# A planner that also books PSUM banks when it works backwards, and three more units turned on TensorE

## The chip, the core and the metric

The program runs on one core of one Trainium2 chip. The engines are TensorE (PE in the profile, with its weight loads as PEld), VectorE (DVE), ScalarE (ACT), GpSimd (POOL) and SyncE (SP, which here only issues transfers). The metric is the device time of one execution in microseconds, as a median of several runs. For the kernel before it is 1066.04 us over three runs (1065.69 to 1067.02).

## The reference, cut to what matters

Three layers follow one another. The first is a linear recurrence over 768 time steps for 4 batches of 8 heads, with a complex decay per channel; the second and third are feed-forward layers over the 3072 tokens that come out of it, the third behind a root-mean-square norm.

```python
mag = np.sqrt(a_re * a_re + a_im * a_im)
scale = np.minimum(mag, 0.999) / (mag + 1e-06)
a_re_n, a_im_n = (a_re * scale, a_im * scale)
for t in range(S):                                   # 768
    new_re = ar * S_re - ai * S_im
    new_im = ar * S_im + ai * S_re
    S_re, S_im = (new_re + k_t (x) v_t, new_im)      # 48 x 48 per batch and head
    y[:, :, t] = q_t @ S_re
x = y as 3072 x 384
h = x @ w_in                                         # 384 x 2048
g = np.where(h >= 1, h, np.where(h <= -1, 0.0, (h + 1) ** 2 / 4))
x = g @ w_out                                        # 2048 x 384
xn = x / sqrt(mean(x * x) + 1e-06) * rms_g
g, val = xn @ w_gate, xn @ w_val                     # 384 x 1536 each
out = (g * sigmoid(g) * val) @ w_out2                # 1536 x 384
```

## The kernel before, in words

The 3072 tokens are cut into 12 **units**: two pairs of batches times six chunks of 128 time steps. A unit has two halves b = 0 and 1, one for each batch of its pair, so 256 tokens. Every float32 product is made of three float16 products (high by high, high by low, low by high), so that each tile has a high and a low part (`wi_h`, `wi_l`, `gmh`, `gml` and so on).

A unit passes through these stages:

- **The chain** (`attn`, up to `chain = plan.stage`): the decays of 128 steps are normalised and multiplied up to running products, channels by rows. ACT squares the input (`X<-a`), then DVE does some 70 to 90 instructions on `X`, `pr`, `C`, `K`, `E` and ends with two products and two sums (`a<-X,E`, `X<-a`). There is one tile `X`, so the chain of a unit cannot begin before the unit ahead of it has been read out of `X`.
- **The transposes of X** (`onto_tokens`): six float32 transposes on PE for each half, `bank<-idt,X`. Those of half 1 are the last reader of `X`.
- **Factors, scores, y, state**: DVE and ACT make k and q with their decays (`qhi`, `qlo`, `khi`, `klo`). These are turned, either by a DMA transpose from SP's queue or by a product with minus the identity on PE (`turned`: `bank<-nid,khi`, then an ACT copy `khT<-bank`). Then PE makes scores, `y` and the state of the recurrence. The result is split (`nh`, `nl`) and turned into `xTh`, `xTl`.
- **M1 and M2** (`moe1`, `moe2`): the two feed-forward layers. Each has a first product into a PSUM bank (`bank<-xTh,wi_h` for M1, `bank<-xnh,wv` for M2), an activation by ACT and DVE ending in `gmh` and `gml`, and a second product into an accumulator (`acc<-wo_h,gmh`, `acc<-w,gmh`).

In the first fifth of the run the weights arrive as 64-bit floats and are decoded by DVE, split by ACT and PE (`wv<-w`, `spt<-w`, `tmp<-spt` on DVE; `bank<-wv,idt`, `bank<-spt,w` on PE). Later, ACT reads the weights once more for range checks (`spt<-spt,e`).

No engine chooses its order at run time. A recorded program of operations is planned by `Plan.best`, and every engine then runs its list in order. The planner works in three steps. `order` is a list scheduler: it walks forward in time and gives each engine the ready operation that is due first (`op.late`); it also hands out the PSUM banks and the `tmp` buffers (`SHARED`), in turns by use and within the limits `CAPS`. `latest` is the backward walk that sets the due times: it runs the plan from its end with the durations of `cost`. In the kernel before, `latest` knows nothing of banks and buffers. `best` repeats the two `ROUNDS` times (once before) and adds a table of offsets, `SHIFT`, by stage name. `PEW` is a table that says for which units which step is done on PE instead of elsewhere: `'add'` means that the last sum of the chain is done by PE, which adds two float32 products in the bank (unit 1 before); `'k'` is the low part of k by PE; `'t'` is the turning of q and k, `'x'` of the layer input and `'n'` of the normed input on PE. `RATES`, `AHEAD1`, `STEP1`, `STEP2` and `CHECKS` set how the operations are interleaved when they are recorded, which decides ties and turns.

All operations are issued from one line (456 in the profile of the kernel before), so in the profile one goes by tile names.

Of the kernel before, what the change touches and what calls it, by code (L numbers as in the profile page):

```python
# [45 lines left out]
}  # L46
TOKS = 2

PEW = {'add': [1], 'sum': [], 'k': [2], 'q': [], 'p': [], 'g': [], 'm': [], 't': [0], 'x': [], 'n': []}

SHIFT = {'w1a': 12, 'm23': 12, 't40': -12, 'm22': 2, 'w2': 25, 't30': -1, 'c2': 3, 'y21': 5, 'c3': -1}
ORDER = [(1, 0), (1, 1), (2, 0), (2, 1), (1, 2)]
RATES = [14.7, 0, 40.2, 27.7, 29.4]
RATE = 0.62
AHEAD1, STEP1, STEP2 = 4, 5, 6
LAG = 3
CHECKS = 12
SWITCH = 8
BACKLOG = 1.5
SHARED = ('bank', 'tmp')  # L60
CAPS = {'mo': 4, 'at': 4, 'w': 4, 'n': 2, 'mo_': 3, 'at_': 3, 'w_': 2, 'out_': 1, 'one_': 1}
ROUNDS = 1
LAT = {'V': 0.13, 'A': 0.145, 'G': 0.1, 'T': 0.0, 'S': 0.0}
XLAT = {'V': 0.13, 'A': 0.145, 'G': 0.1, 'T': 0.2, 'S': 0.0}

# [9 lines left out]
def kw_rows(args, kw):  # L75
    return args[1].shape[0] / P
# [6 lines left out]
class Plan:  # L83
# [92 lines left out]
    def add(self, variants):  # L176

        keys = list(variants)
        name, args, kw = variants[keys[0]]
        aps = [(i, x) for i, x in enumerate(args) if hasattr(x, "ap") and hasattr(x, "offset")]  # L180
        outs = [kw["out"]] if "out" in kw else []
        ins = [x for n, x in kw.items() if n not in ("out", "accum_out") and hasattr(x, "ap") and hasattr(x, "offset")]
        for i, x in aps:
            (outs if i == 0 and "out" not in kw else ins).append(x)
        if kw.get("accum_out") is not None:
            outs.append(kw["accum_out"])
        if name == "matmul" and not kw["start"]:
            ins.append(outs[0])
        n = 1
        for d in list((outs[0]).shape)[1:]:  # L190
            n *= d
        alts = {key: self.cost(key, x[0], n, x[1], x[2], ins) for key, x in variants.items()}
        calls = {key: [x] for key, x in variants.items()}
        table = {AF.Abs_reciprocal_sqrt: 1, AF.Silu: 2}.get(args[2]) if name == "activation" else None
        mm = None
        if "T" in variants:
            f32 = args[1].dtype == F32
            mm = (300 if name == "transpose" else 6 + n * (4 if f32 else 1), kw_rows(args, kw))
        port = sum(x.space != PSUM for x in ins) > 1
# [55 lines left out]
    def cost(key, name, n, args, kw, ins):  # L255
# [12 lines left out]
            return 0.06 + n * {"tensor_tensor": 2.12e-3, "scalar_tensor_tensor": 3.75e-3, "memset": 1.1e-3}.get(name, 3.6e-3)  # L268
        if key == "T":
            f32 = args[1].dtype == F32  # L270
            return 0.4167e-3 * (300 if name == "transpose" else 6 + n * (4 if f32 else 1))
        return 1.25 if "transpose" in name else 0.4

    def best(self):
# [24 lines left out]
    def latest(self, res):  # L299

        ops = self.ops
# [2 lines left out]
            prio[i] = t + ops[i].alts[k]  # L304
        left = [len(op.succs) for op in ops]
        ready = [0.0] * len(ops)
        free = {k: 0.0 for k in self.engines}
        wait_q = {k: [] for k in self.engines}
        av_q = {k: [] for k in self.engines}
        eng = [next(iter(op.alts)) for op in ops]  # L310
        for op in ops:
            if not left[op.idx]:
                heapq.heappush(wait_q[eng[op.idx]], (0.0, op.idx))
        n = 0
        while n < len(ops):
# [12 lines left out]
                heapq.heappush(a, (-prio[i], i))  # L328
            if not a:
                continue  # L330
            op = ops[heapq.heappop(a)[1]]
            n += 1
            c = op.alts[k]
            st = t + (op.dma + 2.0 if op.dma else 0.0) + c
            free[k] = t + max(op.dma, c) if op.dma else st
            op.late = -st
            for p in op.preds:
                ready[p] = max(ready[p], st + (LAT[eng[p]] if eng[p] == k else XLAT[eng[p]]))
                left[p] -= 1
                if not left[p]:  # L340
                    heapq.heappush(wait_q[eng[p]], (ready[p], p))
        first = min(op.late for op in ops)
        for op in ops:
            op.late -= first

    def products(self, op, t):

# [8 lines left out]
    def order(self):  # L356
# [22 lines left out]
        while len(res) < len(ops):  # L379
# [22 lines left out]
                late, i = heapq.heappop(a)  # L402
            op = ops[i]
            new = [v for v in op.tiles if v not in held]
            lack = [v[0] for v in new if not spare[v[0]]] + [v[3] for v in new if turns.get(v[3], 0) != v[4] or using.get(v[3], 0) >= CAPS[v[3]]]
            if lack:
                stuck.setdefault(lack[0], []).append(i)
                continue
# [1042 lines left out]
```

## Time and profile before

| | kernel before |
|---|---|
| median of three runs | 1066.04 us |
| the profiled execution's own time | 1067.5 us |
| span of the profiled execution | 1065.8 us |
| PE busy | 995.5 us, 93% |
| DVE busy | 817.2 us, 77% |
| ACT busy | 812.7 us, 76% |
| mean granted clock of TensorE | 0.974 |

The span is the time from the first to the last instruction; the execution's own time is 1.7 us longer. Busy shares are averages over very different stages. In the first 200 us the weights are prepared; from about 360 us on, one unit after another goes through the same stages until the chain work runs out.

### The profile page before, as it was taken

The numbers are of one execution on the slowest core, as the hardware profiler recorded it, in microseconds if no ns is written. First come the engines' busy times: TensorE is split into PE (matmuls) and PEld (weight loads), VectorE is DVE, ScalarE is ACT, GpSimd is POOL, SyncE is SP. The second block draws the span as 40 slices with busy tenths as digits, with TensorE's granted clock in tenths as the row PEclk, the third lists the DMA queues.
The fourth block names the chain that finished last, engine by engine and source line by source line (L and its number), as shares of the span: only waits on it lengthen the run. The fifth ranks groups of instructions, "written<-read, shape, count | busy, mean of one in ns | idle before, by whom it ended". The sixth has DMA issues, their size and how long they took to land.

```text
span 1065.8 us, 23000 instructions
## 1 busy us (share of the span) xinstructions
PE 995.5 (93%) x9224; PEld 775.2 (73%) x9224; DVE 817.2 (77%) x1721; ACT 812.7 (76%) x1585; POOL 16.7 (2%) x27
## 2 busy tenths in 40 slices
PE   3577998998997899999999999999999999999996
PEld 1355866876875688778777787787887787877874
DVE  9989889979869889698797697896996984633321
ACT  6469879867787798899877897978978989946221
POOL 2000000000000000000000000000000000000000
PEclk9878998999998999999999999999999999999999
DMA  7563265256444443444335526336444321210000
GB/s 255 193 208 121 48 192 138 73 148 159 130 105 123 118 126 94 138 107 105 103 90 147 141 62 168 84 102 169 108 132 139 78 73 36 48 24 16 16 9 26
DMA packets 156018, 115.87 MB, mean 109 GB/s; under 512 B 135296, under 2 KB 138368, under 8 KB 155904
## 3 DMA queue, kind: packets, MB, share of 16 engines
q1 hardware_dynamic: 155904, 114.33, 40.0%
q8 instruction: 74, 1.21, 0.4%
q14 instruction: 40, 0.33, 0.1%
HBM read 77.07 MB, written 4.72 MB: 77 GB/s over the span
## 4 chain that ended last, share of the span: by engine, by line
PE 68%; DVE 16%; ACT 7%; DMA 4%; issue 4%; POOL 0%; SPq 0%; DVEq 0%; ACTq 0%
PE bank L456 43%; PE acc L456 25%; DVE tmp L456 3%; DVE X L456 3%; DVE pr L456 2%; ACT tmp L456 2%; DVE wv L456 2%; DMA w<-in_moe_w_out_dram 1%; ACT L456 1%; DMA spt<-in_moe_w_in_dram 1%; DVE gml L456 1%; DMA qvk<-in_qvk_t_dram 1%; ACT S L456 1%; DVE a L456 1%; ACT X L456 1%
## 5 line engine op out<-in xcount | busy, mean ns | idle before, releaser
L456 DVE SCALAR_TENSOR_TENSOR tmp<-bank,tmp 128x512 f32<-128x512 f32 (+1 forms) x184 | 117.0, 639 | 102.9 <-ACT tmp L456 56.2
L456 PEld LDWEIGHTS <-gmh 128*128 128x128 f16 x1344 | 130.1, 98 | 76.4 <-issue 10.6
L456 PE MATMUL bank<-xTh,wi_h 128*128 128x256 f16 (+1 forms) x672 | 169.1, 262 | 5.2 <-DVE S L456 2.6
L456 PE MATMUL bank<-xTl,wi_h 128*128 128x256 f16 (+1 forms) x672 | 169.0, 262 | 0.3 <-DMA xTl<-nl 0.3
L456 PE MATMUL bank<-xTh,wi_l 128*128 128x256 f16 (+1 forms) x672 | 169.0, 262 | 0.0
L456 ACT ACTIVATE gmh<-tmp 128x512 f16<-128x512 f32 (+1 forms) x184 | 107.5, 588 | 64.7 <-DVE tmp L456 50.4
L456 PE MATMUL bank<-xnh,wv 128*128 128x256 f16 x864 | 155.2, 273 | 0.0
L456 PEld LDWEIGHTS <-wi_h 128*128 128x128 f16 x1344 | 127.2, 100 | 27.1 <-issue 5.8
L456 PE MATMUL acc<-w,gmh 128*128 128x384 f16 x576 | 140.6, 326 | 1.9 <-DVE nl L456 0.7
L456 PEld LDWEIGHTS <-wv 128*128 128x128 f16 x1296 | 126.5, 98 | 16.7 <-issue 0.7
L456 PE MATMUL acc<-wo_h,gmh 128*128 128x384 f16 x384 | 126.5, 329 | 3.6 <-ACT tmp L456 3.6
L456 PE MATMUL acc<-wo_h,gml 128*128 128x384 f16 x384 | 126.3, 329 | 1.8 <-DVE gml L456 1.8
L456 PE MATMUL acc<-wo_l,gmh 128*128 128x384 f16 x384 | 126.5, 329 | 0.0
L456 ACT ACTIVATE tmp<-tmp 128x512 f32<-128x512 f32 (+1 forms) x224 | 124.7, 565 | 2.1
L456 PE MATMUL bank<-xnl,wv 128*128 128x256 f16 x432 | 117.7, 273 | 0.0
L456 PE MATMUL bank<-xnh,wg_l 128*128 128x256 f16 x432 | 117.7, 273 | 0.0
L456 PE MATMUL bank<-xnl,wg_h 128*128 128x256 f16 x432 | 117.7, 273 | 0.0
L456 PE MATMUL bank<-xnh,wg_h 128*128 128x256 f16 x432 | 117.7, 273 | 0.0
L456 PEld LDWEIGHTS <-gml 128*128 128x128 f16 x672 | 66.0, 98 | 47.5 <-DVE gml L456 2.6
L456 PEld LDWEIGHTS <-wg_h 128*128 128x128 f16 x864 | 84.1, 98 | 16.1 <-issue 1.1
L456 PE MATMUL acc<-w,gml 128*128 128x384 f16 x288 | 93.9, 326 | 0.0
L456 ACT ACT_TABLE_LOAD x67 | 86.0, 1283 | 4.9 <-DMA spt<-in_moe_w_in_dram 3.0
(185 smaller groups left out, 2192.1 us busy)
## 6 DMA issues: line engine op xcount, KB each, us to landing
qvk<-in_qvk_t_dram SPq DMA_DIRECT2D x24, 576.0 KB
spt<-in_moe_w_out_dram SPq DMA_DIRECT2D x14, 768.0 KB
a<-in_a_ch_dram SPq DMA_DIRECT2D x12, 768.0 KB
w<-in_moe_w_in_dram SPq DMA_DIRECT2D x12, 512.0 KB
w<-in_moe_w_out_dram SPq DMA_DIRECT2D x8, 768.0 KB
w<-in_moe_w_gate_dram SPq DMA_DIRECT2D x6, 768.0 KB
w<-in_moe_w_val_dram SPq DMA_DIRECT2D x6, 768.0 KB
spt<-in_moe_w_out_dram SPq DMA_DIRECT2D x12, 384.0 KB
```

The source lines that it names most:

```text
L456: getattr(self.engines[k], name)(*args, **kw)
```

## The change

Four things are edited. `latest` now books tiles of banks and buffers when it walks backwards, by the same turns and limits as `order` (the test is moved into a shared function `lacking`). The walk is repeated four times instead of once. The planner's cost of a transpose rises from 300 to 320 cycles and a product costs at least 61 cycles. And the tables change: `PEW` gives units 0, 1 and 3 the turning of q and k by PE (only unit 0 before), and unit 0 the turning of its layer inputs; the last sum of unit 1's chain goes from PE to DVE; the low part that PE makes is that of q in unit 1 instead of k in unit 2. `SHIFT`, `RATES`, `CAPS` and the recording steps get other numbers, and the range checks are recorded earlier.

```diff
-PEW = {'add': [1], 'sum': [], 'k': [2], 'q': [], 'p': [], 'g': [], 'm': [], 't': [0], 'x': [], 'n': []}
+PEW = {'add': [], 'sum': [], 'k': [], 'q': [1], 'p': [], 'g': [], 'm': [], 't': [0, 1, 3], 'x': [0], 'n': [0]}
...
-CHECKS = 12
+CHECKS = 4
...
-CAPS = {'mo': 4, 'at': 4, 'w': 4, 'n': 2, 'mo_': 3, 'at_': 3, 'w_': 2, 'out_': 1, 'one_': 1}
-ROUNDS = 1
+CAPS = {'mo': 3, 'at': 5, 'w': 4, 'n': 2, 'mo_': 3, 'at_': 2, 'w_': 2, 'out_': 1, 'one_': 1}
+ROUNDS = 4
...
-            mm = (300 if name == "transpose" else 6 + n * (4 if f32 else 1), kw_rows(args, kw))
+            mm = (320 if name == "transpose" else max(61, 6 + n * (4 if f32 else 1)), kw_rows(args, kw))
...
+        users, spare, held, stuck, turns, using = {}, {}, set(), {}, {}, {}
         for op in ops:
+            for v in op.tiles:
+                users[v] = users.get(v, 0) + 1
+                spare.setdefault(v[0], [0.0] * v[2])
+                turns[v[3]] = max(turns.get(v[3], 0), v[4])
...
-            op = ops[heapq.heappop(a)[1]]
+            i = heapq.heappop(a)[1]
+            op = ops[i]
+            new = [v for v in op.tiles if v not in held]
+            lack = self.lacking(new, spare, turns, using)
+            if lack:
+                stuck.setdefault(lack[0], []).append(i)
+                continue
+            when = max([spare[v[0]][0] for v in new], default=0.0)
+            if when > t + 1e-9:
+                heapq.heappush(w, (when, i))
+                continue
...
+    @staticmethod
+    def lacking(new, spare, turns, using):
+
+        return ([v[0] for v in new if not spare[v[0]]] +
+                [v[3] for v in new if turns.get(v[3], 0) != v[4] or using.get(v[3], 0) >= CAPS[v[3]]])
```

Since the planner decides the order, the change moves instructions on every engine. The kinds and counts change little. On PE there are 152 products with the identity of 128 columns more (`bank<-nid,...`) and 12 float32 products of unit 1's sum fewer, while another 12 of these become plain transposes. DVE has two instructions more. ACT has 40 more, all of them copies out of a bank behind the turning. SP issues 24 DMA transposes fewer.

On DVE, where unit 1's chain ends, its last sums stood in the program before as follows (`X_105` and `a_0_104` are the tiles `X` and `a`, `E_108` the running product of the groups, `tmp`, `gml` and `bank` belong to unit 0's M1):

```order
L456 TENSOR_TENSOR a_0_104<-X_105,E_108 128x1536
L456 SCALAR_TENSOR_TENSOR tmp_125<-bank_122,tmp_125 128x256
L456 TENSOR_TENSOR X_105<-X_105,E_108 128x1536
L456 SCALAR_TENSOR_TENSOR tmp_128<-bank_115,tmp_128 128x256
L456 SCALAR_TENSOR_TENSOR fl_140<-St_88,sc_0_86 128x3
```

In the changed program the same place on DVE reads:

```order
L490 TENSOR_TENSOR a_0_104<-X_105,E_108 128x1536
L490 SCALAR_TENSOR_TENSOR tmp_148<-bank_115,tmp_148 128x256
L490 TENSOR_TENSOR X_105<-a_0_104 128x768
L490 SCALAR_TENSOR_TENSOR tmp_102<-bank_119,tmp_102 128x256
L490 TENSOR_TENSOR a_0_104<-X_105,E_108 128x1536
L490 SCALAR_TENSOR_TENSOR gml_150<-tmp_148,gmh_149 128x256
L490 TENSOR_TENSOR X_105<-a_0_104 128x768
```

The two sums `X<-a`, which PE formed in the bank before, are now DVE's own.

On DVE, at the end of unit 4's chain, the low part `nl` of unit 3's second half (from which M1 of unit 3 gets its input) stood behind the running products and behind the first large product of the chain:

```order
L456 TENSOR_TENSOR K_0_110<-pr_106 128x12
L456 TENSOR_TENSOR pr_106<-C_107,K_109 128x2x72 x2
L456 TENSOR_TENSOR E_108<-pr_106 128x3x4x6 x2
L456 TENSOR_SCALAR E_108<-E_108 128x96
L456 TENSOR_SCALAR fx_144<-St_88 128x1
L456 TENSOR_TENSOR a_0_104<-X_105,E_108 128x1536
L456 SCALAR_TENSOR_TENSOR nl_143<-bank_115,fx_144,nh_142 128x384
L456 TENSOR_TENSOR X_105<-a_0_104 128x768
```

Now it stands ahead of them (tile numbers have shifted: `nl_142` is the same part of the same half):

```order
L490 TENSOR_SCALAR fx_143<-St_88 128x1
L490 SCALAR_TENSOR_TENSOR tmp_102<-bank_115,tmp_102 128x512
L490 TENSOR_TENSOR C_107<-pr_106 128x2x24
L490 SCALAR_TENSOR_TENSOR gml_153<-tmp_125,gmh_152 128x512
L490 TENSOR_TENSOR pr_106<-C_107 128x4x24
L490 SCALAR_TENSOR_TENSOR nl_142<-bank_116,fx_143,nh_141 128x384
L490 TENSOR_TENSOR C_107<-pr_106 128x2x24
L490 SCALAR_TENSOR_TENSOR gml_155<-tmp_102,gmh_154 128x512
L490 TENSOR_TENSOR pr_106<-C_107,K_109 128x4x6
L490 SCALAR_TENSOR_TENSOR vl_112<-qvk_113,fl_117,vh_111 128x384
```

Unit 3's input no longer waits behind the end of unit 4's chain.

On PE, the transposes of unit 4's first half (`bank<-idt,X`) stood in the program before right behind a second product of unit 2's M1 and ahead of the first product of unit 3's M1:

```order
L456 LDWEIGHTS gml_157
L456 MATMUL acc_0_162<-wo_h_69,gml_157 128x384
L456 MATMUL bank_122<-idt_81,X_105 128x128 x3
L456 MATMUL bank_116<-idt_81,X_105 128x128 x3
L456 LDWEIGHTS wi_h_67
L456 MATMUL bank_103<-xTh_145,wi_h_67 128x256
```

Now they stand behind the state product of unit 3's second half, and behind the first 54 products of its M1:

```order
L490 LDWEIGHTS klo_0_96
L490 MATMUL bank_115<-vh_111,klo_0_96 128x48
L490 MATMUL bank_116<-idt_81,X_105 128x128 x3
L490 MATMUL bank_120<-idt_81,X_105 128x128 x3
L490 LDWEIGHTS wi_h_67
L490 MATMUL bank_124<-xTh_144,wi_h_67 128x256
```

Between the last transpose of unit 3 and the first of unit 4, PE had 528 rows before and has 808 rows now.

## Rows read from the trace of the kernel before

**Rows 1.** The page, part 1: busy time and share of the span, PE to POOL.
```profile
PE 995.5 (93%) x9224; PEld 775.2 (73%) x9224; DVE 817.2 (77%) x1721; ACT 812.7 (76%) x1585; POOL 16.7 (2%) x27
```

**Rows 2.** By stretch: PE, PEld, DVE, ACT, POOL busy (count); PEclk, DMA, GB/s.
```profile
0.00:100.00 100.00, 58.49 (x330) 36.61 (x331) 93.41 (x188) 64.47 (x135) 6.49 (x13) 0.83 0.59 199
100.00:185.00 85.00, 78.78 (x870) 63.51 (x868) 76.40 (x175) 69.58 (x172) 0.86 (x1) 0.96 0.48 124
...
320.00:360.00 40.00, 31.11 (x262) 21.06 (x261) 37.27 (x87) 27.42 (x59) 0.70 (x1) 0.88 0.45 125
360.00:1050.00 690.00, 688.77 (x6472) 547.90 (x6470) 497.21 (x1012) 543.96 (x1009) 6.51 (x9) 1.00 0.36 92
```

**Rows 3.** The chain that ended last, at 507: start, length, what.
```profile
507.06 1.95 PE acc L456 x12
509.01 1.96 PE bank L456 x18
```

**Rows 4.** PE in time: start, length, instruction; first and last of 24 scores.
```profile
307.26 0.22 PE L456 MATMUL bank<-qhT,khT 96*128 96x128 f16 x1
...
308.55 0.22 PE L456 MATMUL bank<-qhT,klT 96*128 96x128 f16 x1
```

**Rows 5.** PE in time at 119, unit 1's sum for one half.
```profile
119.49 2.91 PE L456 MATMUL bank<-idt,X 128*128 128x128 f32 x12
122.23 2.84 PE L456 MATMUL bank<-idt,a 128*128 128x128 f32 x12
124.91 0.33 PE L456 MATMUL acc<-wo_h,gmh 128*128 128x384 f16 x1
```

**Rows 6.** PE in time at 493: a half's transposes, and what follows.
```profile
493.26 1.06 PE L456 MATMUL bank<-idt,X 128*128 128x128 f32 x6
494.16 0.27 PE L456 MATMUL bank<-xnh,wg_h 128*128 128x256 f16 x1
```

**Rows 7.** From q's low part to its first product: units 0, then 1.
```profile
L456 DVE TENSOR_TENSOR qlo<-qvk,qhi x2: 948/948/949, 61.6 to 88.9; 128x768 f16<-128x768 f32 x2
L456 PE MATMUL bank<-qlT,khT x8: 216/219/314, 73.9 to 75.2; 96*128 96x128 f16 x8
L456 DVE TENSOR_TENSOR qlo<-qvk,qhi x1: 951/951/951, 127.6 to 127.6; 128x768 f16<-128x768 f32 x1
L456 PE MATMUL bank<-qlT,khT x16: 217/219/219, 142.6 to 175.0; 96*128 96x128 f16 x16
```

**Rows 8.** A copy behind the turning: busy us, mean ns of one.
```profile
L456 ACT ACTIVATE khT<-bank 96x512 f16<-96x512 f32 x4 | 2.1, 580 | 0.0
```

**Rows 9.** PE's waits, 253 to 357: idle time before, and its releaser, in brackets.
```profile
258.55 0.20 PE L456 MATMUL bank<-vh,ph 128*128 128x48 f16 x1 [1.33 <-ACT ph L456]
259.56 0.20 PE L456 MATMUL bank<-vh,pl 128*128 128x48 f16 x1 [0.78 <-DVE pl L456]
330.24 0.34 PE L456 MATMUL acc<-wo_h,gml 128*128 128x384 f16 x1 [1.76 <-DVE gml L456]
334.69 0.48 PE L456 MATMUL acc<-wo_h,gmh 128*128 128x384 f16 x1 [3.63 <-ACT tmp L456]
356.42 1.08 PE L456 MATMUL bank<-idt,X 128*128 128x128 f32 x6 [2.20 <-DVE X L456]
```

**Rows 10.** Tile X, 314 to 358, unit 4: min/median/max ns, first and last start.
```profile
L456 PE MATMUL bank<-idt,X x12: 298/300/401, 316.3 to 357.2; 128*128 128x128 f32 x12
L456 DVE TENSOR_TENSOR X<-a x2: 947/948/949, 351.9 to 355.4; 128x768 f32<-128x768 f32 x2
```

**Rows 11.** Tile X, 448 to 496, unit 6.
```profile
L456 PE MATMUL bank<-idt,X x12: 298/300/381, 449.8 to 494.0; 128*128 128x128 f32 x12
L456 DVE TENSOR_TENSOR X<-a x2: 945/948/952, 488.2 to 492.2; 128x768 f32<-128x768 f32 x2
```

**Rows 12.** Tile X, 598 to 651, unit 8.
```profile
L456 PE MATMUL bank<-idt,X x12: 272/300/379, 599.1 to 649.2; 128*128 128x128 f32 x12
L456 DVE TENSOR_TENSOR X<-a x2: 946/948/950, 640.8 to 645.0; 128x768 f32<-128x768 f32 x2
```

More of the change, by code (lines that the diff above doesn't have):

```diff
@@ L47 @@
 TOKS = 2
-PEW = {'add': [1], 'sum': [], 'k': [2], 'q': [], 'p': [], 'g': [], 'm': [], 't': [0], 'x': [], 'n': []}
-SHIFT = {'w1a': 12, 'm23': 12, 't40': -12, 'm22': 2, 'w2': 25, 't30': -1, 'c2': 3, 'y21': 5, 'c3': -1}
+PEW = {'add': [], 'sum': [], 'k': [], 'q': [1], 'p': [], 'g': [], 'm': [], 't': [0, 1, 3], 'x': [0], 'n': [0]}
+SHIFT = {'m21': 1, 't20': 6, 'w1b': -3, 'w2a': 1}
 ORDER = [(1, 0), (1, 1), (2, 0), (2, 1), (1, 2)]
-RATES = [14.7, 0, 40.2, 27.7, 29.4]
-RATE = 0.62
-AHEAD1, STEP1, STEP2 = 4, 5, 6
+RATES = [10.7, 0, 34.2, 40.7, 32.4]
+RATE = 0.67
+AHEAD1, STEP1, STEP2 = 6, 6, 6
 LAG = 3
-CHECKS = 12
+CHECKS = 4
 SWITCH = 8
@@ L270, in cost @@
             f32 = args[1].dtype == F32
-            return 0.4167e-3 * (300 if name == "transpose" else 6 + n * (4 if f32 else 1))
+            return 0.4167e-3 * (320 if name == "transpose" else max(61, 6 + n * (4 if f32 else 1)))
         return 1.25 if "transpose" in name else 0.4
@@ L306, in latest @@
         ready = [0.0] * len(ops)
+        eng = [next(iter(op.alts)) for op in ops]
         free = {k: 0.0 for k in self.engines}
@@ L309, in latest @@
         av_q = {k: [] for k in self.engines}
-        eng = [next(iter(op.alts)) for op in ops]
+        users, spare, held, stuck, turns, using = {}, {}, set(), {}, {}, {}
         for op in ops:
+            for v in op.tiles:
+                users[v] = users.get(v, 0) + 1
+                spare.setdefault(v[0], [0.0] * v[2])
+                turns[v[3]] = max(turns.get(v[3], 0), v[4])
             if not left[op.idx]:
@@ L330, in latest @@
                 continue
-            op = ops[heapq.heappop(a)[1]]
+            i = heapq.heappop(a)[1]
[9 more added lines that the diff above has]
+                continue
+            for v in new:
+                held.add(v)
+                heapq.heappop(spare[v[0]])
+                turns[v[3]], using[v[3]] = v[4] - 1, using.get(v[3], 0) + 1
+                for j in stuck.pop(v[3], ()):
+                    heapq.heappush(wait_q[eng[j]], (max(ready[j], t), j))
             n += 1
@@ L336, in latest @@
             op.late = -st
+            for v in op.tiles:
+                users[v] -= 1
+                if not users[v]:
+                    heapq.heappush(spare[v[0]], st + XLAT[k])
+                    using[v[3]] -= 1
+                    for j in stuck.pop(v[0], []) + stuck.pop(v[3], []):
+                        heapq.heappush(wait_q[eng[j]], (max(ready[j], st + XLAT[k]), j))
             for p in op.preds:
@@ L404, in order @@
             new = [v for v in op.tiles if v not in held]
-            lack = [v[0] for v in new if not spare[v[0]]] + [v[3] for v in new if turns.get(v[3], 0) != v[4] or using.get(v[3], 0) >= CAPS[v[3]]]
+            lack = self.lacking(new, spare, turns, using)
             if lack:
```

## The prediction

> **What bounds the kernel now.** I read four views in this order. The busy shares first: TensorE (PE) is busy 93% of the span, VectorE 77%, ScalarE 76% [rows 1]. The stretches next, since an average hides stages. From 360 to 1050 us PE is busy 688.77 of 690 us at full clock: there the end moves only by PE's own work, or by a wait that is new. From 0 to 100 us PE is busy 58.49 us and VectorE 93.41, from 100 to 185 us they stand at 78.78 and 76.40 of 85, so the start belongs to both in turns, VectorE first. From 320 to 360 us PE is busy 31.11 of 40 us at a clock of 0.88, while VectorE is busy 37.27 [rows 2]. Third, the chain that ended last shows PE's price where it never waits: 12 products of 384 columns in 1.95 us (0.1625 each) and 18 of 256 in 1.96 us (0.109 each) [rows 3]; 24 scores of 128 columns start from 307.26 to 308.55, 23 steps of 0.056 us [rows 4]. Products of 48 columns I price by their columns at 0.02 us, an estimate from the last. Fourth, the waits and tile `X` show why PE starves near 340 us: the chain of unit 4 runs from the transposes that free `X` (316.3) to its last sum (355.4 + 0.95 = 356.4), 40.1 us, and the product behind it starts at 356.42 [rows 9, 10].
>
> The profiled execution took 1067.5 us, 1.5 more than the median. The sum is made against the former; the predicted median is 1.5 lower.
>
> **PE's own work.** 152 turning products of 128 columns come: 152 x 0.056 = +8.5 us. Unit 1's sum on PE cost, for one half, 119.49 to 124.91 = 5.42 us [rows 5] (each f32 product stands there as two). Twelve plain transposes remain of the two halves, and six take 493.26 to 494.16 = 0.90 us [rows 6]. So -(10.84 - 1.8) = -9.0 us. Together -0.5 us. VectorE takes over four sums of 0.95 us [rows 10], but its list grows by two instructions only. At the start, where the clock is 0.83 to 0.96, these prices are low by up to that share; I leave that to the next term.
>
> The trace's 0.056 us for 128 columns is that of a run in which each weight load serves one product [rows 4]. The Trainium skill (TensorE: Matmul & The Clock Gate, section "Back-to-back issue gap") says that a stream of weight loads with a 128-column product each keeps to about 81 ns a product. By that the turning would cost 152 x 0.081 = 12.3 us and the whole forecast would be 3.8 us later; the trace speaks against it.
>
> **The start.** In the changed order VectorE has 34 more instructions ahead of the last half-split that unit 1's M1 needs from it in the recorded list (much of it the chain of unit 2, put earlier); at 76.40 / 175 = 0.44 us [rows 2] that is 15 us. PE has about 10 us more products there less half of what unit 1's sum gives back, so after that point some 5 us less to do. If VectorE sets this point, the end moves by 15 - 5 = +10 us less what VectorE's idle time takes up; from 100 to 185 it idles 85 - 76.4 = 8.6 us [rows 2]. That leaves +1.4 to +10. If PE sets it, the start is worth nothing beyond PE's -0.5. One thing speaks for less idle time: between q's low part and its first product unit 0, turned by PE, took 61.6 to 73.9 = 12.3 us with VectorE's weights in between, and unit 1, by DMA, 127.6 to 142.6 = 15.0 [rows 7]; unit 1 now goes PE's way. I take +3.5, the middle of the two cases' near ends and half of VectorE's idle time. Bounds: -3 (the 2.7 us of unit 1 saved as well) and +10.
>
> The 24 DMA transposes fewer and the 40 copies more (0.58 us each, 23 us [rows 8]) I cost at nothing: ScalarE is idle 15.4 of 85 us there [rows 2], in three places of some 13 copies each. If that cover is gone, it delays the scores of units 0, 1 and 3 by a few copies each, 2 us at one place; that is inside the bounds.
>
> **Unit 2's y.** PE waited 1.33 and 0.78 us for `ph` and `pl` of the state [rows 9]. The changed order has 33 products of 256 columns' worth (3.6 us) between score and y instead of 1.3 us, which covers it: -1.5, between 0 and -2.1.
>
> **Unit 4's hand-over.** This is the large term. Between the last transposes of unit 3 and the first of unit 4 PE's list holds 96 products of 384 columns, 72 of 256, 24 of 128 and 72 of 48: 15.6 + 7.8 + 1.3 + 1.4 = 26.2 us, with the transposes' own 0.9 some 27. The chain needs 40.1 [rows 10]. So 13 us are lost, which the waits (1.76 + 3.63 + 2.20 [rows 9]) and the half clock that followed them (40 x 0.12 = 4.8 us [rows 2]) about make up. The changed list holds 105, 171, 56 and 72: 17.1 + 18.6 + 3.1 + 1.4 = 40.3, with transposes 41.2. The chain has 79 VectorE instructions instead of 73: 6 x 37.27 / 87 = +2.6 [rows 2], so 42.7 needed and 1.5 lost. Gain 13 - 1.5 = 11.5; I take -12 with a little for the clock. What is late next is the same `X`, by 1.5 us. The bounds are -13.7 (all idle time and lost clock of that stretch) and -4 (if unit 3's first half comes as late as it did and the extra work stands in the wrong half).
>
> **The later hand-overs.** Work put in front of unit 4 is missing behind it. For units 5 to 11 the same reading of tile `X` gives needs of 45.4, 43.3, 45.7, 46.9, 45.9, 44.3 and 45.2 us; two are shown: unit 6 from 449.8 to 493.1, with the transposes at 493.26 [rows 6, 11], and unit 8 from 599.1 to 645.95, 2.6 us ahead of its transposes at 648.6 [rows 12]. PE's work in between was 44.5, 43.0, 49.3, 48.9, 46.9, 45.0 and 48.9 us with transposes, so all but nothing was lost. Now it is 40.1, 42.1, 44.7, 41.6, 42.0, 46.0 and 45.1. The chains change by -11, +3, +3, -7, -10, -4 and +2 VectorE instructions at 497.21 / 1012 = 0.49 us [rows 2], so the needs become 40.0, 44.8, 47.2, 43.5, 41.0, 42.3 and 46.2: short by 0, 2.7, 2.5, 1.9, 0, 0 and 1.1, together 8.2, against 1.2 before: +7. VectorE idles 28% of this stretch, so part of a need is a wait for PE that shrinks with it. I take +5. Bounds: 0, and +15 if the instructions taken out of the chains leave its length as it was.
>
> **The sum.** -0.5 + 3.5 - 1.5 - 12 + 5 = -5.5: 1062.0 us for an execution like the profiled one, and a median of 1060.5.
>
> **Rivals.** (1) The later hand-overs stay hidden, since the needs give way, and PE sets the start: -0.5 + 0 - 1.5 - 12 + 1 = -13, 1053. For it: VectorE's 28% of idle time; against: unit 6 was just in time before and has 1 us less of PE work now.
> (2) Slower: the later hand-overs bite. PE stands at the transposes of units 6, 7, 8 and 11 with its list used up, as it stood at unit 4's, and each such wait costs clock besides. With +13 there and +8 at the start: -0.5 + 8 - 1.5 - 12 + 13 = +7, 1073. It decides from where these two terms pass 14 us together. For it: four of seven units now have less PE work than chain; against: before, units 5 and 6 were short by this reckoning too and lost next to nothing (1.2 of 690 us idle).
> (3) The gain at unit 4 only moves: unit 3's second half frees `X` no earlier than now, so that unit 4 still ends near 356 and PE waits ahead of unit 3's M1 instead. Then that term is -6: 1066. For it: VectorE is at 93% from 320 to 360 [rows 2], and its list up to this point is no shorter; against: VectorE's list has the input of unit 3 earlier there.
> (4) The turning costs what the skill's sentence says: 1064. Only unit 0's turning stands in the trace, at low clock.
>
> **How the numbers follow.** Forecast 0.42, rival 1 0.20, rival 2 0.18, rival 3 0.16, rival 4 0.04. A measurement here can tell about 0.2%, 2.1 us, from no change. Faster: the forecast with 0.36 of its 0.42, rival 1 whole, 0.03 of rivals 3 and 4: 0.59. Same: 0.05 of the forecast, 0.13 of the rivals: 0.18. Slower: rival 2, the tail of rival 3 and of the forecast: 0.23. The range goes from 1050 (rival 1 with a better start) to 1072, just short of rival 2's middle. The forecast's own range is 1056 to 1065.
>
> **What would show it.** Right: PE's wait of 2.20 us for `X` and the two M1 waits near 330 us gone or under 2 us together; the clock of that stretch near 1; the transposes of unit 4's first half 7 to 10 us earlier than 356.4; PE's idle time from 360 to 1050 up from 1.2 us to some 4 to 6, ended by `X` at units 6, 7, 8 and 11. Rival 2 would show waits of 3 us and more there with a clock under 1; rival 3 unit 4's transposes at 354 or later. The start is read from unit 1's first transposes, before at 119.49 [rows 5], and from unit 3's last, before at 316.3 [rows 10], which the moved work alone would bring to 306: later than 310 says that VectorE set the start. What would make it wrong outright is a wait that no row of before shows, such as for a bank now that the turns of the banks are others.

## The result, and the profile after

The changed kernel takes 1051.26 us (median of four runs, 1049.39 to 1052.02) against 1065.87 for the kernel before on the same chip: ratio 0.986, 95% interval 0.9843 to 0.9877. That is 14.6 us faster. The forecast was 1060.5, 5.5 us faster: the direction was right, the size was not, and 1051.3 lies near the low end of the range. The profiled execution took 1050.8 us, its span is 1049.1; the profiled one of the kernel before took 1067.5, so those two, which the forecast's sum is made for, are 16.7 us apart.

The busy rows of the page after (part 1; busy us, share of the span, instructions):

```profile
span 1049.1 us, 23263 instructions
PE 989.0 (94%) x9340; PEld 773.3 (74%) x9340; DVE 814.9 (78%) x1723; ACT 829.3 (79%) x1625; POOL 21.7 (2%) x27
```

The same stretches as in [rows 2], after (columns as there; the last one ends 20 us earlier, since the run does):

```profile
0.00:100.00 100.00, 58.98 (x357) 38.22 (x358) 96.25 (x196) 69.89 (x149) 6.49 (x13) 0.86 0.60 205
100.00:185.00 85.00, 79.06 (x906) 60.81 (x904) 81.68 (x203) 78.70 (x190) 4.20 (x1) 0.94 0.32 99
320.00:360.00 40.00, 38.18 (x369) 29.91 (x368) 36.93 (x88) 35.09 (x74) 0.70 (x1) 1.00 0.35 91
360.00:1030.00 670.00, 667.97 (x6307) 531.60 (x6306) 482.40 (x990) 534.13 (x986) 7.76 (x9) 1.00 0.37 93
```

From 320 to 360 us PE is busy 38.18 us instead of 31.11 and the clock is whole. In the first 185 us VectorE is busy 177.9 us instead of 169.8, while PE's busy time hardly differs (138.0 and 137.3).

PE's own waits from 185 us to 1040, before and then after (total, times, longest):

```profile
PE acc L456 <- ACT tmp L456: 4.3, 2, 3.6
PE bank L456 <- DVE X L456: 2.2, 1, 2.2
PE bank L456 <- DVE pl L456: 2.1, 3, 1.2
PE acc L456 <- DVE gml L456: 1.8, 1, 1.8
PE bank L456 <- ACT ph L456: 1.3, 1, 1.3
...
```

```profile
PE acc L490 <- DVE nl L490: 1.8, 1, 1.8
PE bank L490 <- DVE pl L490: 1.3, 2, 0.8
PE acc L490 <- DVE gml L490: 1.2, 2, 0.6
PE bank L490 <- DVE tmp L490: 0.2, 1, 0.2
```

The waits for `X`, for ScalarE's `tmp` and for `ph` [rows 9] are gone, and the longest wait that is left is 1.8 us.

For the rest I use one measure for all kernels: **PE's lost time** at a point of the program. It is the time at which a half's transposes start, less the price of all products ahead of them, each priced as it runs where PE waits for nothing (0.056, 0.109 and 0.1625 us for 128, 256 and 384 columns [rows 3, 4], 0.133 for a transpose at full clock, 0.225 for each f32 entry of unit 1's sum [rows 5], and 0.025 for 48 columns, the step that most of them have in the trace, where I had estimated 0.02). Waits, half clock and gaps all end up in it. PE's own work is thus counted and priced, not timed. The points are unit 2's second transposes, unit 3's second, unit 5's first and unit 11's second; the time between two of them is the work plus what is lost there.

| | before | after | difference | forecast |
|---|---|---|---|---|
| PE's own work, whole run | 961.2 | 960.6 | -0.6 | -0.5 |
| lost up to unit 2's second transposes | 72.7 | 71.4 | -1.3 | +3.5 |
| from there to unit 3's second | 4.3 | 0.1 | -4.2 | -1.5 |
| from there to unit 5's first (unit 4's hand-over) | 15.9 | 4.2 | -11.7 | -12 |
| from there to unit 11's second | 2.1 | 4.2 | +2.1 | +5 |
| sum (the last product starts at 1058.1 and 1042.3; the other 0.9 us of the 16.7 fall behind it) | | | -15.7 | -5.5 |

The large term came out as forecast. Three others were each too pessimistic: by 4.8, 2.7 and 2.9 us.

### The profile page after: what moved, and what is told of

Read it like the earlier page. It is cut to its first block, busy times and chain, and to the rows that moved or that the text cites. A ratio compares the mean times of both kernels' runs of the same rounds, so it can differ in the third digit from the quotient of the medians.

```text
span 1049.1 us, 23263 instructions
## 1 busy us (share of the span) xinstructions
PE 989.0 (94%) x9340; PEld 773.3 (74%) x9340; DVE 814.9 (78%) x1723; ACT 829.3 (79%) x1625; POOL 21.7 (2%) x27
## 4 chain that ended last, share of the span: by engine, by line
PE 80%; DVE 10%; ACT 4%; DMA 2%; issue 2%; SPq 0%; ACTq 0%; DVEq 0%
PE bank L490 52%; PE acc L490 28%; DVE X L490 2%; DVE wv L490 2%; DMA w<-in_moe_w_in_dram 1%; DVE pr L490 1%; DVE S L490 1%; ACT tmp L490 1%; DVE spt L490 1%; DMA qvk<-in_qvk_t_dram 1%; DVE qvk L490 1%; DVE tmp L490 1%; ACT X L490 1%; DMA spt<-in_moe_w_in_dram 1%; ACT S L490 0%
## 5 line engine op out<-in xcount | busy, mean ns | idle before, releaser
L490 ACT ACTIVATE gmh<-tmp 128x512 f16<-128x512 f32 (+1 forms) x184 | 107.3, 588 | 51.5 <-DVE tmp L490 44.8
L490 PEld LDWEIGHTS <-wg_h 128*128 128x128 f16 x864 | 84.4, 98 | 14.8 <-issue 0.2
```

The lines of the kernel that those rows point to most:

```text
L490: getattr(self.engines[k], name)(*args, **kw)
```

## The experiments

Each kernel below was run in several rounds beside the kernel before. "Lost" has the four parts of the table above.

**What each part of the change is worth.** Seven kernels are the changed one with a single part undone, and one is the kernel before with the new walk in four rounds. The plan is made anew each time. The title's "three more units" are two, as `PEW` shows: the turning of q and k comes to units 1 and 3, 64 products each; the other 24 of the 152 turn the layer inputs of unit 0.

`a_pewold`:
```diff
-PEW = {'add': [], ..., 'k': [], 'q': [1], ..., 't': [0, 1, 3], 'x': [0], 'n': [0]}
+PEW = {'add': [1], ..., 'k': [2], 'q': [], ..., 't': [0], 'x': [], 'n': []}
```


> The changed kernel with the table of PE's extra work (PEW) as before: unit 0 alone turned by PE, unit 1's last sum on PE, the new planner and tables kept. Changed kernel 1051.3, before 1066. Theory P (the planner's new due times carry the gain): at most 1056, and PE's lost time up to unit 2's first transposes stays near 71 us. Theory W (the work moved to and from PE carries it): 1061 or more, with unit 2's transposes back near 205 us. Unit 1's sum on PE alone gives 9 us of PE work back; if PE sets the start, that appears in the time.

`a_oldwalk` (the body of `latest` as before, `lacking` kept for `order`):
```diff
-            lack = self.lacking(new, spare, turns, using)
-            if lack:
-                stuck.setdefault(lack[0], []).append(i)
-                continue
...
```


> The changed kernel with the old backward walk, which knows no banks, still four rounds. Theory P (due times that know the banks carry the gain): 1061 or more, and unit 4's hand-over again with about 40 us of chain over less than 30 us of PE work. Theory W (the moved work carries it): at most 1056.

`a_tabold`: SHIFT, RATES, RATE, the recording steps, CHECKS and CAPS with the numbers of the kernel before.


> The changed kernel with the old numbers in SHIFT, RATES, RATE, the recording steps, CHECKS and CAPS. Theory T (the hand-fitted numbers carry the gain): 1061 or more. Theories P and W: at most 1056. The old numbers were fitted to another plan, so some loss speaks for none of them.

`b_walk4` (the kernel before with the new `latest`):
```diff
-ROUNDS = 1
+ROUNDS = 4
```


> The kernel before with the new backward walk (it books banks) in four rounds, and nothing else. Theory P: at most 1059, with unit 4's hand-over covered. Theories W and T: 1064 to 1068, or slower, since the old numbers were fitted to the old due times.

`a_rounds1`:
```diff
-ROUNDS = 4
+ROUNDS = 1
```


> The changed kernel with the backward walk done once instead of four times. Theory D (due times from one walk still fit a plan that is then given up, so several hand-overs miss): 1060 or more, with PE's loss spread over two or more units' transposes. Rival E (one walk is enough, the booking of banks does it): within 3 us of 1051.3.

`a_turn03` and `a_noxn`:
```diff
-..., 't': [0, 1, 3], ...
+..., 't': [0, 3], ...
```
```diff
-..., 'x': [0], 'n': [0]}
+..., 'x': [], 'n': []}
```


> The changed kernel with unit 1's q and k turned by DMA again (units 0 and 3 stay on PE): 64 products of 128 columns fewer, 3.6 us of PE work. VectorE's waits in the first 210 us fell from 15.3 us before to 7.3 us in the changed kernel. Theory W1 (turning unit 1 on PE is what took them away, through the wait of qvk for ACT, 5.6 us before): they are 12 us or more again, PE's lost time up to unit 2's second transposes goes from 71.4 to 75 or more, and the time is 1056 or more. Rival O (the order took them away): waits under 10 us, 1048 to 1053.

> The changed kernel with the layer inputs of unit 0 turned by DMA as before (24 products of 128 columns fewer, 1.3 us of PE work). Theory W2 (these turnings freed the queue from which the weights come, so VectorE's waits for weights fell from 4.0 to 0.5 us): the waits for weights are 3 us or more again, PE's lost time up to unit 1's second transposes rises from 59.6 to 62 or more, 1054 or more. Rival O: within 2 us of 1051.3.

`a_add1`:
```diff
-PEW = {'add': [], ...
+PEW = {'add': [1], ...
```


> The changed kernel with the last sum of unit 1's chain on PE again, everything else kept and planned anew: PE gets 9 us of work back near 120 to 153 us, VectorE loses two sums. Theory V (VectorE sets that stretch, so PE's 9 us are hidden): within 4 us of 1051.3. Rival P: 6 to 9 us slower. A new plan can lose more than either, as the first four runs showed; which it is shows in PE's lost time up to unit 2's first transposes (71 us now).

| kernel | median us | ratio to before, interval | work | lost in the four parts |
|---|---|---|---|---|
| before | 1066.0 | 1 | 961.2 | 72.7, 4.3, 15.9, 2.1 |
| changed | 1051.3 | 0.986 (0.9843 to 0.9877) | 960.6 | 71.4, 0.1, 4.2, 4.2 |
| a_pewold | 1069.4 | 1.0036 (1.0022 to 1.005) | 961.2 | 76.4, 1.5, 15.9, 3.3 |
| a_oldwalk | 1086.3 | 1.0185 (1.016 to 1.021) | 960.6 | 76.3, 7.4, 14.3, 18.3 |
| a_tabold | 1070.5 | 1.0035 (1.0023 to 1.0048) | 960.6 | 77.7, 0.3, 14.7, 6.5 |
| b_walk4 | 1068.4 | 1.0016 (1.0005 to 1.0027) | 961.2 | 75.9, 2.7, 10.5, 7.2 |
| a_rounds1 | 1068.2 | 1.0015 (1.0005 to 1.0026) | 960.6 | 71.9, 0.7, 14.3, 9.3 |
| a_turn03 | 1077.0 | 1.0097 (1.0076 to 1.0119) | 957.0 | 85.8, 1.4, 9.2, 11.8 |
| a_noxn | 1064.9 | 0.9989 (0.9976 to 1.0001) | 959.3 | 76.9, 0.2, 10.7, 7.7 |
| a_add1 | 1071.6 | 1.0049 (1.0032 to 1.0066) | 969.7 | 74.7, 1.5, 11.0, 6.6 |

No part carries the gain in time: with any one of them undone all or nearly all of it is gone. (The planner's two new costs, 320 and 61 cycles, were never undone alone.) Theories P, W and T, each of which gave the gain to one part, are all refuted: P by `a_pewold`, which was to stay under 1056, and by `b_walk4` (1059), W by `a_oldwalk` and `a_tabold`, and T, which `a_tabold` alone would bear out, by `a_pewold` and `a_oldwalk`, which keep its numbers. In `a_oldwalk` P's time came true but not its place: unit 4's hand-over has 43 us of PE work there, and most of the loss falls on units 3, 5, 6 and 7. `a_rounds1` bears out theory D: with one walk the loss is spread over units 4, 5 and 6. The new walk in four rounds, with the old tables, takes 5.4 us off the third part (15.9 to 10.5) and gives them back before and behind. Of these kernels only the changed one keeps all of the last three parts at 4.2 us or less.

The third part holds two hand-overs, units 4 and 5, and taken singly they say more. Ahead of unit 4's first transposes alone PE loses 12.7 us before and 2.1 in the changed kernel; it loses 13.4 in `a_pewold`, 8.6 in `b_walk4`, and 1.5 to 4.0 in the other six, whose lists hold 39.0 to 43.1 us of PE's work there (27.4 before, 31.0 in `a_pewold`, 36.2 in `b_walk4`). So unit 4's term does hang on one part, the table of PE's extra work. Of its entries unit 1's turning, unit 0's layer inputs and unit 1's sum were undone singly without losing it; unit 3's turning and the low parts of q and k were not. What the other six lose instead lies between unit 4's second transposes and unit 5's first (6.0 to 8.8 us, 0.1 in the changed kernel) and, in all but `a_rounds1`, at the start too (74.7 and more). In the expectation for `a_add1` theory V had PE's 9 us hidden; PE's work did rise by 9.1 us, the start's loss rose too (71.4 to 74.7), and 20 us came in all. The rival's 6 to 9 us were also wrong, since a new plan came with the edit.

`a_turn03` gave W1 its 1056 or more and its 75 or more, but not by the wait it named: VectorE's wait of `qvk` for ScalarE stays at 0.6 us, although its waits in the first 210 us add up to 14.8 us again. With unit 1 turned by DMA, PE waited for the DMA that turns M1's input (`xTh`) and for splits; none of its waits between 150 and 210 us is for the turning of q or k itself:

```profile
PE bank L490 <- DMA xTh<-nh: 2.5, 1, 2.5
PE bank L490 <- ACT nh L490: 2.4, 1, 2.4
PE acc L490 <- DVE nl L490: 2.2, 1, 2.2
PE bank L490 <- ACT qlo L490: 2.2, 1, 2.2
...
```

`a_noxn` gave W2's time, 1054 or more, and its loss at unit 1 (63.1 instead of 59.6), but the waits for weights stayed at 0.8 us: that mechanism is refuted too. Which edit removed VectorE's waits stays open; neither of these two did it in the way it named.

**Unit 2's chain.** Five kernels move or lengthen it. Three give the planner another offset (`b_c2m20` that of the kernel before), the other two keep the changed kernel's order and repeat instructions when they are issued.

`a_c2p20`, `a_c2p40` and `b_c2m20`:
```diff
-SHIFT = {'m21': 1, 't20': 6, 'w1b': -3, 'w2a': 1}
+SHIFT = {'c2': 20, 'm21': 1, 't20': 6, 'w1b': -3, 'w2a': 1}
```
```diff
-SHIFT = {'m21': 1, 't20': 6, 'w1b': -3, 'w2a': 1}
+SHIFT = {'c2': 40, 'm21': 1, 't20': 6, 'w1b': -3, 'w2a': 1}
```
```diff
-SHIFT = {..., 'c2': 3, ...}
+SHIFT = {..., 'c2': -20, ...}
```


> The changed kernel, with unit 2's chain alone told to be 20 us less urgent. On VectorE its two large products then end behind four more low parts of M1 (place 418 of the list instead of 401), some 7 us later. Theory X (the end follows the time at which unit 2's chain is through, 192 us now, 205.6 before; each later chain up to unit 5 hangs on it): 6 to 8 us slower, 1057 to 1060, and unit 5's transposes as much later as unit 2's. Theory H (what counts is that PE has work over unit 4's chain): within 2 us of 1051.3, since that stretch of PE's list stays as it is.

> The kernel before, with unit 2's chain alone told to be 20 us more urgent instead of 3 less. Its large products end behind 25 low parts of M1 instead of 29 (place 418 instead of 423), some 2 to 3 us earlier. Theory X: 2 to 3 us faster than 1066. Theory H: no change, since unit 4's hand-over stays short of PE work.

> The changed kernel with unit 2's chain told to be 40 us less urgent: its large products end at place 449 of VectorE's list instead of 401, some 20 us later. With 20 us of shift the end had come 5.8 us later at unit 2's transposes and the kernel was 2.3 us faster, since PE had 9 us more of M1 to do ahead of them. Theory L (what counts is whether PE has work left at each transpose, and M1 of unit 1 ends there): 8 to 14 us slower than the changed kernel, lost at the transposes of units 2 or 3. Rival R (unit 2's chain has room): 1047 to 1052.

`a_dupchain2`, and `a_dupbehind2` in the same way for 11 `gml`:
```diff
-                    getattr(self.engines[k], name)(*args, **kw)
+                    again = 0
...
+                        if o == "X" and a == "a2" and list(args[0].shape) == [128, 768]:
+                            sums += 1
+                            again = 3 if sums in (5, 6) else 0
+                    for _ in range(1 + again):
+                        getattr(self.engines[k], name)(*args, **kw)
```


> The changed kernel, same order, with the two last sums of unit 2's chain done four times instead of once: 6 x 0.95 = 5.7 us more of VectorE inside that chain, near 190 us. Theory X: 4.5 to 5.7 us slower, 1056 to 1057. Theory H: 0 to 2 us slower, since from unit 3 on PE has as much work as the chains need.

> The changed kernel, same order, with the next 11 low parts of M1 behind unit 2's chain done twice: 5.4 to 5.7 us more of VectorE, as in the run with the doubled sums, but between unit 2's chain and unit 3's (192 to 225 us). Theory X: at most 3 us slower, since VectorE has slack between the chains and only what is left delays unit 3's. Theory H, and theory V (VectorE's total work up to unit 5 sets the time): as much as in the other run.

| kernel | median us | ratio to before, interval | unit 2's first transposes | lost in the four parts |
|---|---|---|---|---|
| changed | 1051.3 | 0.986 (0.9843 to 0.9877) | 192.0 | 71.4, 0.1, 4.2, 4.2 |
| a_c2p20 | 1048.9 | 0.9836 (0.982 to 0.9852) | 197.8 | 67.9, 1.7, 4.2, 4.3 |
| a_c2p40 | 1071.7 | 1.0055 (1.0038 to 1.0072) | 215.2 | 64.9, 18.5, 6.4, 10.2 |
| a_dupchain2 | 1058.2 | 0.9924 (0.9908 to 0.9941) | 196.7 | 78.3, 0.1, 4.3, 4.3 |
| a_dupbehind2 | 1053.8 | 0.9881 (0.9865 to 0.9898) | 190.5 | 72.5, 0.6, 4.3, 4.6 |
| b_c2m20 | 1081.7 | 1.014 (1.0123 to 1.0157) | 201.3 | 73.2, 2.9, 29.3, 3.9 |

Theory X fell on its first test. In `a_c2p20` unit 2's transposes came 5.8 us later and the kernel was no slower, because 9.1 us more of PE's products (130.0 instead of 120.9 by then) stood ahead of the transposes. Theory H fell on the next: 5.7 us of VectorE inside the chain with nothing more for PE to do cost 7.0 us, far over its 0 to 2, and the wait stands where it should, in the trace of `a_dupchain2`:

```profile
196.69 1.54 PE L498 MATMUL bank<-idt,X 128*128 128x128 f32 x6 [5.31 <-DVE X L498]
```

The same work behind the chain cost 2.5 us, inside X's bound of 3, where theories H and V had as much as in the other run. So a chain may end late as long as PE has products to do until then; theory L says this, and `a_c2p40` shows the other end of it. There 33 us of products were moved ahead of unit 2's first transposes (154.0 instead of 120.9), PE lost 10 us less up to them, and then it had nothing left, in the trace of `a_c2p40` near 250 us:

```profile
248.11 0.48 PE L490 MATMUL bank<-w,nid 128*128 128x384 f16 x1 [6.02 <-ACT w L490]
257.56 0.80 PE L490 MATMUL acc<-w,gmh 128*128 128x384 f16 x2 [7.37 <-DVE nl L490]
```

It was 20 us slower than the changed kernel, more than L's 8 to 14. In `b_c2m20` unit 2's first transposes came 4.3 us earlier, unit 4's at 356.4 as before, and then PE's list had unit 4's scores next and waited for their turning by DMA; it was 15.6 us slower than the kernel before, where theory X had 2 to 3 us faster and theory H no change:

```profile
368.75 0.29 PE L456 MATMUL bank<-qhT,khT 96*128 96x128 f16 x1 [10.80 <-DMA khT<-khi]
```

**Does VectorE set the start, and do its waits take up work?** Two kernels repeat weight decodes, in the order of before and of after.

`b_dupstart` and `a_dupstart` (decodes 24 to 29 and 25 to 30):
```diff
-                    getattr(self.engines[k], name)(*args, **kw)
+                    again = 0
...
+                            decodes += 1
+                            again = 2 if 25 <= decodes <= 30 else 0
+                    for _ in range(1 + again):
+                        getattr(self.engines[k], name)(*args, **kw)
```


> The kernel before, same order, with six of VectorE's weight decodes between 113 and 158 us done three times: 12 x 0.55 = 6.6 us more of VectorE. Theory V (VectorE sets the start, and its waits there, 8.6 us between 100 and 185 before, take up added work): 0 to 3 us slower. Rival P (PE sets the stretch up to 205 us, VectorE has room): within 1 us. Rival S (VectorE's waits take up nothing, each is one of a chain): 5 to 7 us slower.

> The changed kernel, same order, with six of VectorE's weight decodes between 109 and 147 us done three times: 12 x 0.55 = 6.6 us more of VectorE, which waits only 3.3 us between 100 and 185 there. Theory V: 4 to 6.6 us slower. Rival P: within 1 us. Rival S: 5 to 7 us slower.

Measured: 1071.5 us, ratio 1.0045 (1.0029 to 1.0062), and 1056.1, ratio 0.9904 (0.9883 to 0.9924): about 5 us slower each, for 6.6 us of VectorE. Rival P is refuted: VectorE sets this stretch in both kernels. By the times theory V just misses for the kernel before (at most 3, where the interval has 3.1 to 6.6) and holds for the changed one; with rival S's 5 to 7 it is the other way round. The traces tell more. Up to the start of unit 1's last split (`nl<-bank,fx,nh`, from which its M1 gets its input), in `b_dupstart` and then in `a_dupstart` (columns as in [rows 2]):

```profile
0.00:184.00 184.00, 133.63 (x1161) 98.06 (x1162) 172.51 (x366) 130.88 (x295) 7.35 (x14) 0.88 0.55 164
0.00:186.10 186.10, 135.59 (x1213) 95.19 (x1214) 180.78 (x391) 145.71 (x328) 10.70 (x14) 0.93 0.45 152
```

Without the repeated decodes the split starts at 180.8 and 181.3, behind 165.6 and 174.4 us of VectorE's work (the rows stand in the next section). So VectorE has 6.9 and 6.4 us more to do, its idle time is 3.7 and 1.6 us less, and the split comes 3.2 and 4.8 us later. The waits of the kernel before do take up a part of added work, and more of it than those of the changed kernel. Where the other 1.8 us of `b_dupstart`'s 5.0 arise is not settled.

**Are the later hand-overs just in time?** `a_duplate` repeats the last sums of units 5 to 11.
```diff
...
+                            again = 2 if sums >= 11 else 0
...
```


> The changed kernel, same order, with the two last sums of the chains of units 5 to 11 done three times: 4 x 0.95 = 3.8 us more of VectorE at the end of each of seven chains, 26.6 us in all. In the trace of the changed kernel these chains end 0.1 to 0.6 us ahead of their transposes. Theory N (each later hand-over is just in time, so the chain sets it): 22 to 27 us slower, 1073 to 1078. Rival G (the chains hold waits for PE that shrink): at most 12 us slower.

Measured: 1089.2 us, ratio 1.0204 (1.0182 to 1.0226), 38 us slower than the changed kernel for 26.6 us of VectorE. Rival G is refuted; theory N has the mechanism and too small a price. Of unit 8 in the trace of `a_duplate`, and of the stretch from unit 5's second half on (columns as in [rows 2]):

```profile
650.49 1.08 PE L498 MATMUL bank<-idt,X 128*128 128x128 f32 x6 [3.79 <-DVE X L498]
```

```profile
420.00:1030.00 610.00, 586.00 (x5384) 459.25 (x5382) 447.23 (x893) 476.14 (x875) 6.49 (x8) 0.98 0.36 89
```

Unit 8's 3.8 us at the end of its chain became a wait of PE of 3.8 us. At the transposes of units 5 to 11 PE waits 3.4, 3.7, 3.7, 3.8, 3.6, 3.5 and 2.3 us for `X`, where the changed kernel has no such wait. Over the stretch, which holds the last six of these, PE is idle 24 us of 610, and 2% of the clock, 12 us, goes as well: here the waits cost half as much again in clock.

**Side by side.** 

> The changed kernel once more, beside the next run on the same chip: 1050 to 1052 us.

> The changed kernel with unit 2's chain 20 us less urgent, once more, since it came out 2.3 us faster than the changed kernel in another comparison. If that holds: 1048 to 1050 us and 1.5 to 3 us under the run beside it; if it was chance: within 1 us of it.

Measured: 1050.8 us, ratio 0.9849 (0.9834 to 0.9864), and 1049.8, ratio 0.984 (0.9827 to 0.9854). The difference is 1.0 us here and was 2.3 between separate comparisons; the intervals overlap. Both beat the kernel before, and whether unit 2's chain is better placed 20 us later stays open.

## Why the prediction was right on one term and wrong on the sum

**PE's own work** was forecast as -0.5 and is -0.6. In the changed trace eight turning products in a row, at full clock, take 290.12 to 290.57, 0.056 us each:

```profile
290.12 0.61 PE L490 MATMUL bank<-nid,klo 128*96 128x128 f16 x8
290.57 0.61 PE L490 MATMUL bank<-nid,qhi 128*96 128x128 f16 x8
```

The Trainium skill (TensorE: Matmul & The Clock Gate, section "Back-to-back issue gap") has about 81 ns for 128 columns in a stream of weight loads with one product each; here the trace disagrees, and rival 4 is out.

**The start failed, and it is the largest of the three misses** (4.8 us). The step was: 34 more instructions, 15 us more of VectorE, ahead of the last split that unit 1's M1 needs, less 5 us of PE's work, less what VectorE's idle time takes up. With half of that idle time it gives 15 - 5 - 4.3 = +5.7, with all of it +1.4, and I took +3.5 between them. The last split of unit 1, VectorE's work up to its start and the first products of M1 behind it stand in the traces as follows, before and then after (second row of each: columns as in [rows 2]):

```profile
L456 DVE SCALAR_TENSOR_TENSOR nl<-bank,fx,nh x4: 606/608/611, 87.9 to 180.8; 128x384 f16<-128x384 f32 x4
0.00:180.80 180.80, 133.08 (x1161) 97.23 (x1162) 165.60 (x354) 130.53 (x295) 7.35 (x14) 0.89 0.55 167
L456 PE MATMUL bank<-xTh,wi_h x48: 219/219/219, 186.9 to 199.6; 128*128 128x128 f16 x48
```

```profile
L490 DVE SCALAR_TENSOR_TENSOR nl<-bank,fx,nh x3: 608/614/616, 111.4 to 181.3; 128x384 f16<-128x384 f32 x3
0.00:181.30 181.30, 134.34 (x1213) 96.42 (x1214) 174.41 (x379) 144.89 (x328) 10.69 (x14) 0.90 0.46 156
L490 PE MATMUL bank<-xTh,wi_h x48: 219/219/219, 188.0 to 203.4; 128*128 128x128 f16 x48
```

None of the step's three numbers came out. Ahead of this split VectorE has 26 more instructions (353 and 379), not 34; 34 more stand ahead of another split, the first of unit 0's M2 (325 and 359). They are 8.8 us of work, not 15. VectorE's idle time up to the split is 8.3 us less (15.2 and 6.9), not 4.3. So the split comes 0.5 us later, where the step with half of the idle time had it 10.7 later. M1 of that half starts 1.1 us later, with 2.6 us more of PE's work done ahead of it, not 5. PE's loss up to there falls by 1.5 us, and the term's -1.3 is made up to there.

The gain lies at the very start, where the forecast had no term: up to unit 0's first transposes (56.9 us before, 53.6 now) PE loses 3.4 us less. VectorE was at 93% there, so I took nothing to be won, though two weight decodes fewer (0.95 us each) stand ahead of unit 0's sums in its list, and its waits for weights up to them fell from 1.9 to 0.5 us. From there to unit 2's first transposes PE's loss rose from 31.9 to 33.8 us, by 1.9.

VectorE does set this stretch, as forecast (`b_dupstart`, `a_dupstart`). But its idle time takes up no fixed share of what is added: ahead of the split it took up 3.7 of 6.9 us in one of those two kernels and 1.6 of 6.4 in the other. It consists of waits for particular operands, and which of them there are changes with the order. VectorE's waits in the first 210 us, before and then after:

```profile
DVE qvk L456 <- ACT S L456: 5.6, 5, 1.7
DVE wv L456 <- DMA w<-in_moe_w_out_dram: 3.5, 2, 2.1
DVE tmp L456 <- PE bank L456: 1.5, 1, 1.5
...
```

```profile
DVE spt L490 <- PE bank L490: 1.8, 2, 1.0
DVE gml L490 <- ACT gmh L490: 1.6, 1, 1.6
...
DVE qvk L490 <- ACT S L490: 0.2, 1, 0.2
...
```

All waits of this view add up to 15.4 us before and 7.3 after. With nearly the same number of instructions ahead of unit 1's last split as in the changed kernel (376 to 394, and 379), VectorE's idle time up to it is 10.3 us in `a_noxn`, 14.0 in `a_turn03` and 19.0 in `a_add1`, against 6.9. So the order decides it; by what it does so is not shown.

**Unit 2's y** was forecast as -1.5 from two waits of 2.1 us together; both are gone. The stretch gave 4.2 us: two more short waits of before (0.6 us each, for `tmp` and `w`) and the gaps around them went too. The term was read from the longest rows alone.

**Unit 4's hand-over** was forecast as -12 and gave -11.7. Tile `X` after, 298 to 346 us, answers to [rows 10]:

```profile
L490 PE MATMUL bank<-idt,X x12: 297/300/381, 300.5 to 344.8; 128*128 128x128 f32 x12
L490 DVE TENSOR_TENSOR X<-a x2: 957/958/959, 339.0 to 341.8; 128x768 f32<-128x768 f32 x2
```

The chain took 300.5 to 342.8, 42.3 us (forecast 42.7), beside 41.5 us of PE work (forecast 41.2). The transposes then started without a wait:

```profile
344.05 1.06 PE L490 MATMUL bank<-idt,X 128*128 128x128 f32 x6
```

The forecast had 1.5 us lost there, with `X` late by as much. 2.1 us were lost, but `X` was ready 1.3 us ahead of its transposes, so at most 0.8 of them are the chain's; the near agreement on this remainder is luck. Rival 3 is out: unit 4's transposes start at 344.0 instead of 356.4, unit 3's second at 300.5 instead of 316.3. I had asked for 7 to 10 us earlier at unit 4; the rest is what the start and unit 2's y gave. By the forecast's own sign a start set by VectorE would have put unit 3's second transposes later than 310, and the moved work alone at 306: they came earlier than either, so this sign could not show what sets the start.

**The later hand-overs** were forecast as +5 with seven numbers behind it. Needs, forecast and measured, units 5 to 11: 40.0 and 39.8; 44.8 and 43.1; 47.2 and 44.7; 43.5 and 43.7; 41.0 and 42.0; 42.3 and 45.8; 46.2 and 45.2. So a count of instructions times their mean gives a chain's length within 3.5 us. It was too long at units 6, 7 and 11, where it had PE short of work by 2.7, 2.5 and 1.1 us, and right at unit 8, where 1.9 us were forecast and 1.9 lost. The sign I had asked for did not come: from 360 to 1030 us PE idles 2.0 us, not 4 to 6, and never for `X`; what it loses ahead of units 6 and 8 stands as waits for `pl` and `gml`, shown above. At unit 6 one reason is in the rows: ScalarE's square of the input starts 0.6 us behind the transposes that free `X`, in the trace of after between 436 and 484 us,

```profile
L490 PE MATMUL bank<-idt,X x12: 296/300/380, 438.8 to 482.8; 128*128 128x128 f32 x12
L490 DVE TENSOR_TENSOR X<-a x2: 949/954/959, 477.1 to 480.9; 128x768 f32<-128x768 f32 x2
L490 ACT ACTIVATE X<-a x1: 1483/1483/1483, 439.4 to 439.4; 128x1536 f32<-128x1536 f32 x1
```

and it started 2.1 us behind them before:

```profile
L456 ACT ACTIVATE X<-a x1: 1485/1485/1485, 451.9 to 451.9; 128x1536 f32<-128x1536 f32 x1
```

The changed order of ScalarE was to be seen in the plan, and I had read only VectorE's. At unit 7 the cause of the 2.5 us is not settled.

**The rivals.** The time is rival 1's (1053), not its mechanism. PE does not set the start, and though the needs did give way at units 6, 7 and 11, the later hand-overs are not hidden by slack: every chain of units 5 to 11 ends within 0.1 to 0.6 us of its transposes in the changed kernel, where unit 7's, 8's and 11's had 2.6 to 4.0 us to spare before, and a lengthened chain costs more than it is long. Rival 2 thus had the right mechanism for these units; the plan stops just short of it. Left open is what in the plan brings that about: the kernels with one part undone or done show that no part brings the whole of it by itself.

## What to carry to other kernels

Where one engine waits for a serial chain on another, add up for each hand-over the chain's length and the waiting engine's work beside it; that sum gave the large term within a microsecond. Don't take a fixed share of an engine's idle time as a reserve for added work: ask of each wait which operand it is for, and whether the new order brings that operand earlier. Follow the very tile on which the next stage waits: 34 more instructions were forecast here, and 26 stood ahead of it. And where a planner sets the order, the parts of a change need not have prices that add up: undoing any one of them here lost all of the gain or nearly all.

## What the runs showed of the hardware

An f32 product of 128 columns with a weight of its own was dearer than its columns: 0.225 us for each of its two entries [rows 5], while an f32 product of 384 columns in the same trace takes 0.325 for each of its two (153.66 to 154.31):

```profile
152.77 1.05 PE L456 MATMUL bank<-idt,a 128*128 128x128 f32 x4
153.66 0.81 PE L456 MATMUL bank<-spt,w 128*128 128x384 f32 x2
154.31 0.33 PE L456 MATMUL bank<-wg_h,nid 128*128 128x384 f16 x1
```

And the clock's part of a wait: in `a_duplate` seven waits of 2.3 to 3.8 us, 75 to 88 us apart, each brought a stretch at the lower of the two levels of the clock (1.2 of 2.4 GHz) around its end, as unit 8's, which ended at 650.49, did (columns as in [rows 2]),

```profile
652.00:654.00 2.00, 2.00 (x11) 1.45 (x10) 2.00 (x8) 0.82 (x2) 0.00 (x0) 0.50 0.96 347
```

and the granted clock of 420 to 1030 us was 0.98, 12 us in 610.
